# Gated mix of a memory-augmented recurrent attention and an MLP: the columns of queries and exponentials reordered, the reciprocals of the memory rows kept in PSUM, V's matmuls and the side work regrouped

## The chip, the cores and the metric

The kernel runs on one core of a Trainium2 chip. A core has a matmul engine (TensorE, PE in the profile, its weight loads PEld), a vector engine (VectorE, DVE), an engine for activations and copies (ScalarE, ACT), a general engine (GpSimd, POOL) and one that issues transfers (SyncE, SP). SBUF is the working memory of 128 partitions; PSUM is the memory into which matmuls write, in eight banks of 128 x 512 fp32 values. The engines run side by side, each through its own list of instructions in order, and wait for each other on semaphores.

The metric is the time of one execution on the device in microseconds (us). Before the change, three runs took 794.21, 795.08 and 796.0 us, median 795.08.

## The reference, cut to what matters

A sequence x of 2048 tokens of width 512 goes through two branches, mixed by a gate per token:

```python
g = sigmoid((x * gate_w).sum(-1, keepdims=True))
out = g * A(x) + (1 - g) * B(x)

# B: layernorm, 512 -> 1376, gelu, 1376 -> 512
# A: 64 segments of 32 tokens, 32 heads of 128, a memory of 8 rows that is handed on
mem = mem0
for s in range(64):
    h = concat([mem, x[s * 32:(s + 1) * 32]])          # 40 rows
    q, k, v = h @ Wq, h @ Wk, h @ Wv                    # per head
    p = softmax(where(mask, q @ k.T * scale, -1e9))     # 40 x 40 per head
    o = (p @ v) @ Wo                                    # 40 x 512
    mem = o[:8]
    outs.append(o[8:])
```

The mask lets the 8 memory rows see all 40 rows, and a token sees the memory and the tokens of its segment up to itself. Each segment needs the memory of the one before, so the 64 segments follow one another.

## The kernel before, in words

**Two stages.** The first, up to about 100 us, computes the MLP branch with all 128 tokens of a tile at once, stores (1 - g) * B in DRAM (`c_dr`) and loads the attention's weights into SBUF. The second is a loop over the 64 segments `s`; `T, si = divmod(s, 4)` are its tile of 128 tokens and its place in it. The order of the instructions is written out by hand: each engine does its instructions in the order in which the code issues them, and only the waits are added.

**Rows of a segment.** TensorE multiplies with weights of 32 columns at a time, four such groups side by side, one for each quarter of the output's partitions. So 32 of the 40 rows go together: the 8 memory rows and the first 24 tokens (`RIDE`), in `hT`, transposed. The last 8 tokens (`LEFT`) of the four segments of a tile need no memory for their projections; they are gathered as 32 rows (`GL`) and computed a tile ahead as side work: `QL`, `KL` and `VP` hold their queries, keys and values. `prep_h` and `prep_q`, both on POOL, put the tokens of the next segment into `hT` and the left queries of the next segment into `QT`.

**Projections.** A unit (`qk_unit`, `v_unit`) is four matmuls of 128 x 32 weights by 512 columns, side by side. Q and K take four times four units into the banks `U[0]` to `U[3]`; ScalarE casts each bank (`qk_cast`, line 115) and VectorE transposes it in blocks of 32 into `QT` or `KT` (`qk_tr`, line 119). V takes two times four units into `X1` and `X2`, which ScalarE copies (lines 689 and 702).

**Scores and softmax.** The scores of 16 heads lie in the bank `SbF`, those of the other 16 in `W`, with keys on the partitions and 56 columns (`EW`) for each group of four heads. `mask_mm` first writes the mask there through TensorE (line 248); `scores` adds the products: main keys into columns 8 to 48, left keys into columns 0 to 8 and 48 to 56. Before the change the columns are: 0 to 8 memory queries by left keys, 8 to 16 memory queries by main keys, 16 to 40 the 24 tokens, 40 to 48 left queries by main keys, 48 to 56 left queries by left keys. ScalarE takes the exponentials into `E` (`exps`, line 674), the 16 memory columns first and then the 40 others, each for one block of 16 heads.

**Normalising.** Only the memory rows must be right at once. Their sums come from matmuls with a block of ones (`msum`, into columns 320 to 352 of `U[0]` and `U[1]`); `mnorm` takes the reciprocal into `R` (line 681) and multiplies the memory columns of `E` by it (line 682). The other rows are normalised one segment later: `xsums` forms their sums, turned round, with `E` as the weights, in columns 256 to 264 of `SbF`. As left queries have two parts, it makes two passes of eight matmuls (line 605): one with columns 16 to 48 of `E`, one with `EZ`, a copy of columns 48 to 56 that ScalarE makes behind 24 columns of zeros (line 699). `recip_x` takes the reciprocals (line 616), SP stores them in DRAM (`r_dr`) and loads them back on all partitions (`Rb`), POOL adds `R` to a running sum (`racc`, line 621), and `x_norm` multiplies on POOL (line 629) at the start of the next segment, into columns 8 to 32 of `UT` and into `UL`.

**Back to the memory.** `av` multiplies V by `E` into `U`: first the heads of block 0, then those of block 1 (lines 280 and 285). ScalarE copies the memory columns into `UT` (line 712) and the rest into `XR` (line 611). `wo_pass` multiplies `UT` by `Wo` into the whole bank `W` (line 141), ScalarE copies it to `w` (line 635), four matmuls with the selection `SelM` turn the 8 memory rows (line 724), and VectorE casts them into the next `hT` (line 725). That cast is where the next segment's projections can start; segments are counted here from it.

**Side work.** Each segment has up to eight side units (`side`): projections of the next tile's left tokens at `si` 0, 1 and 3, and `Wo` for the last tile's left tokens at `si` 2. `run(W1)`, `run(W2)` and `run(W3)` issue some of them at three places: ahead of `xsums`, ahead of `wo_pass` and behind it; the rest follow the selection. `extra` adds the transposes of a later tile at `si` 3 and, at `si` 0, `out_sel`: it gathers the finished rows of an earlier tile with four matmuls and one of 128 x 128 weights.

The last tile has no next tile, so its segments 60 and 61 have no side units. The last segment, 63, normalises all rows at once and writes the last tile out. The program also tracks the smallest reciprocal and their sum; a slow general version at its end runs only where these leave their bounds.

Of the kernel before, what the change touches and what calls it, by code (L numbers as in the profile page):

```python
# [9 lines left out]
FP32 = mybir.dt.float32  # L10
# [8 lines left out]
MASK_NEG = -1.0e9  # L19
# [8 lines left out]
def kernel(ctx, tc, A_x, A_mem0, A_Wq, A_Wk, A_Wv, A_Wo, A_seg_len, B_x, B_w1, B_b1, B_w2, B_b2, gate_w, out):  # L28
# [89 lines left out]
    def qk_tr(Tb, dst, hf):  # L118
        nc.vector.transpose(out=dst[:, 8 * hf:8 * hf + 8, 0:32, :].rearrange("p a r b -> p a (r b)").bitcast(FP32),  # L119
                            in_=Tb[:].rearrange("p a e b -> p (a e b)").bitcast(FP32))  # L120
# [103 lines left out]
    def out_sel(T, bk):  # L224
# [3 lines left out]
        nc.tensor.matmul(bk[:], lhsT=SelL[:], rhs=wls.pop(T)[:], start=False, stop=True, skip_group_check=True)  # L228
# [36 lines left out]
    def sums(out, E, c_main, c_left, n, start):  # L265
# [3 lines left out]
        for j in range(4):  # L269
            nc.tensor.matmul(out[32 * j:32 * j + 32, :, n - 8:n], lhsT=BO[:, 32 * j:32 * j + 32], rhs=E[:, :, c_left:c_left + 8],  # L270
                             start=False, stop=True, skip_group_check=True, tile_position=(0, 32 * j))
# [20 lines left out]
    with tc.tile_pool(name="mlpw", bufs=1) as mlpw, \  # L292
# [81 lines left out]
        for c in range(4):  # L374
            nc.gpsimd.affine_select(out=SelM[:], in_=SelM[:], pattern=[[-1, M]], compare_op=ALU.not_equal, fill=1.0, base=-32 * c, channel_multiplier=1)
            nc.gpsimd.affine_select(out=SelI[:], in_=SelI[:], pattern=[[-1, 32]], compare_op=ALU.not_equal, fill=1.0, base=-32 * c, channel_multiplier=1)
# [4 lines left out]
        def consts():  # L381
# [5 lines left out]
            nc.vector.tensor_scalar(out=rf[:, 0:1], in0=rf[:, 0:1], scalar1=float(M), scalar2=None, op0=ALU.subtract)  # L387
            nc.vector.tensor_scalar(out=mk1[:], in0=iof[:, 0:4], scalar1=rf[:, 1:2], scalar2=MASK_NEG, op0=ALU.not_equal, op1=ALU.mult)
            yield
            for a in range(4):  # L390
                nc.vector.tensor_scalar(out=Mk[:, a, 16:16 + RIDE], in0=iof[:], scalar1=rf[:, 0:1], scalar2=MASK_NEG, op0=ALU.is_lt, op1=ALU.mult)
                nc.vector.tensor_copy(out=Mk[:, a, 0:8], in_=mk1[:, a:a + 1].to_broadcast([P, 8]))
                nc.vector.tensor_scalar(out=Mk[:, a, 48:56], in0=iof[:, 0:8], scalar1=rf[:, 2:3], scalar2=MASK_NEG, op0=ALU.is_lt, op1=ALU.mult)
                nc.vector.tensor_scalar(out=Mk[:, a, 48:56], in0=Mk[:, a, 48:56], scalar1=mk1[:, a:a + 1], scalar2=None, op0=ALU.add)
# [85 lines left out]
        def first():  # L480
# [3 lines left out]
            dve_q.append(lambda: nc.vector.tensor_copy(out=hT[0][:, :, 0:M], in_=m0p))  # L484
# [112 lines left out]
    EZ = [lp.tile([P, NG, 32], BF16, name=f"EZ{i}") for i in range(2)]  # L597
    for i in range(2):
        nc.gpsimd.memset(EZ[i][:, :, 0:RIDE], 0.0)

    def xsums(s, E):
        for first, src, c0 in ((True, E, 16), (False, EZ[s % 2], 0)):
            for i in range(NG):
                c, h = i % 4, i // 4
                nc.tensor.matmul(xs8[32 * c:32 * c + 32, 4 * h:4 * h + 4], lhsT=src[:, i, c0:c0 + 32], rhs=BO[:, 0:P:32],  # L605
                                 start=first and h == 0, stop=not first, skip_group_check=True, tile_position=(0, 32 * c))

    def x_raw(s):
        XR = cw.tile([P, 4, NG, 32], BF16, tag="XR", name="XR")
        for j in range(4):  # L610
            nc.scalar.copy(out=XR[:, j], in_=U[j][:, 0:NG * 40].rearrange("p (i q) -> p i q", q=40)[:, :, 8:40])  # L611
        XRs[s] = XR

    def recip_x(s):
# [5 lines left out]
        nc.sync.dma_start(Rb[:].rearrange("p r e -> p (r e)"), r_dr[s % 2][:].rearrange("r e -> (r e)").partition_broadcast(P))  # L620
        nc.gpsimd.tensor_tensor(out=racc[:, 0:RW], in0=racc[:, 0:RW], in1=R[:, 0:RW], op=ALU.add)  # L621
        Rbs[s] = Rb

    def x_norm(s):
        T, si = divmod(s, SPT)
        XR, Rb = XRs.pop(s), Rbs.pop(s)[:].rearrange("p (c q) (h j) -> p h j c q", c=4, h=2)
        for out, o, a, b in ((UT[(s + 1) % 2], M, 0, RIDE), (UL[T % 2], LEFT * si, RIDE, 32)):
# [10 lines left out]
    W1, W2, W3 = 2, 2, 2  # L638
    for s in range(nseg):
        T, si = divmod(s, SPT)  # L640
        last = s == nseg - 1
        hc, hn = hT[s % 3], hT[(s + 1) % 3]
        fill = side(T, si)
# [13 lines left out]
        for n, (t, hf) in enumerate(((0, 0), (1, 0), (0, 1), (1, 1))):  # L657
# [14 lines left out]
        def exps(i2, x):  # L672
            c = slice(16, EW) if x else slice(0, 16)
# [220 lines left out]
```

## Time and profile before

| What | Value |
|---|---|
| Median of three runs | 795.08 us (794.21 to 796.0) |
| The profiled execution's own time | 796.19 us |
| Its span, first to last instruction | 794.4 us |
| Granted TensorE clock | 0.998 |
| First and last cast of line 725 | 109.1 and 774.2 us |
| Busy time of PE, ACT, DVE, POOL | 767.9, 539.9, 327.7, 277.8 us |

The profile is one execution. A line of a timeline has a start from the span's beginning and a length in us, the engine, the line of the code, the operation, what is written and read, and how many equal instructions were merged; brackets hold the engine's idle time before it and what ended it. A merged line's length runs to the end of its last instruction. Matmuls are pipelined, so that one lasts 0.38 us while a new unit starts every 0.216 us.

From the first to the last cast of line 725 there are 62 segments in 665.1 us, 10.73 us each. Most single ones stand between 10.64 and 10.66 us; those with an output selection take 10.85; a few are longer.

### The profile page before, as it was taken

To read this page: it belongs to the slowest core of one execution; us is meant where nothing else is said; L and a number is where in the kernel's file an instruction comes from. 1 tells how busy PE (TensorE), PEld (TensorE's weight loads), DVE (VectorE), ACT (ScalarE), POOL (GpSimd) and SP (SyncE) were. 2 spreads that over 40 slices of the span, in tenths; PEclk is the share of its full clock that TensorE was granted. 3 is DMA by queue.
4 is the path that set the end of the run, shared out by engine and by line. 5 is a ranking of instruction groups with operands and counts; after the bars stand their busy time and mean duration, and the time that the engine had idled before them with its cause. 6 is when DMAs were issued, how large, how long until landed. Compare 5 with 4: busy or idle time off the path is not lost.

```text
span 794.4 us, 42412 instructions
## 1 busy us (share of the span) xinstructions
PE 767.9 (97%) x18921; PEld 428.8 (54%) x18950; DVE 327.7 (41%) x1061; ACT 539.9 (68%) x1503; POOL 277.8 (35%) x519
## 2 busy tenths in 40 slices
PE   7999999999999999999999999999999999999996
PEld 5666555555555555555555555555555555555553
DVE  4776344333334343434343333434343434333334
ACT  3666676766777676767776677777677767776663
POOL 3111033343344434234334324443334434332332
PEclk9999999999999999999999999999999999999999
DMA  6779411212111222211121212122221212121211
GB/s 189 265 269 350 142 59 58 74 60 86 60 53 68 77 70 70 77 57 60 60 86 61 86 61 75 46 75 70 78 70 57 62 58 86 61 80 60 71 65 36
DMA packets 46723, 70.49 MB, mean 89 GB/s; under 512 B 12799, under 2 KB 36456, under 8 KB 45000
## 3 DMA queue, kind: packets, MB, share of 16 engines
q1 hardware_dynamic: 45016, 64.97, 25.0%
q8 instruction: 150, 2.46, 1.3%
q0 software_dynamic: 720, 1.97, 0.7%
q10 hardware_dynamic: 800, 0.79, 0.3%
q14 instruction: 37, 0.30, 0.1%
HBM read 59.06 MB, written 4.45 MB: 80 GB/s over the span
## 4 chain that ended last, share of the span: by engine, by line
PE 93%; ACT 4%; issue 1%; DVE 1%; DMA 1%; POOL 0%; SPq 0%; DVEq 0%; POOLq 0%; ACTq 0%
PE U L110 28%; PE X L129 18%; PE W L141 14%; PE X L110 7%; PE U L468 5%; PE U L280 4%; PE X L141 3%; ACT w L635 3%; PE W L462 3%; PE SbF L462 3%; PE W L724 2%; PE U L267 1%; PE SbF L605 1%; PE SbF L256 1%; PE W L248 1%
## 5 line engine op out<-in xcount | busy, mean ns | idle before, releaser
L629 POOL TENSOR_TENSOR UT<-XR,Rb 128x384 bf16<-128x384 bf16 x126 | 140.0, 1132 | 271.8 <-DMA Rb<-r_dr 211.7
L115 ACT CAST Tb<-U 128x512 bf16<-128x512 f32 x258 | 151.0, 585 | 83.2 <-PE U L110 82.7
L110 PEld LDWEIGHTS <-hT 128*32 128x32 bf16 x4096 | 103.9, 97 | 109.7 <-DVE hT L725 19.1
L110 PE MATMUL U<-Wq_sb,hT 128*32 128x512 bf16 x2048 | 132.8, 379 | 1.1 <-DVE hT L725 1.1
L129 PE MATMUL X<-Wv_sb,hT 128*32 128x512 bf16 x2048 | 133.2, 378 | 0.0
L110 PE MATMUL U<-Wk_sb,hT 128*32 128x512 bf16 x2048 | 132.7, 379 | 0.0
L141 PE MATMUL W<-Wo_sb,UT 128*32 128x512 bf16 x2080 | 124.6, 380 | 1.5 <-ACT UT L712 1.2
L725 DVE CAST hT<-W 128x32 bf16<-128x32 f32 x63 | 12.1, 192 | 231.2 <-PE W L724 231.2
L119 DVE STREAM_TRANSPOSE QT<-Tb 128x256 f32<-128x256 f32 x128 | 57.0, 445 | 82.2 <-ACT Tb L115 81.1
L141 PEld LDWEIGHTS <-UT 128*32 128x32 bf16 x2080 | 57.2, 96 | 58.0 <-POOL racc L621 19.0
L119 DVE STREAM_TRANSPOSE KT<-Tb 128x256 f32<-128x256 f32 x128 | 57.0, 445 | 58.2 <-ACT Tb L115 58.2
L611 ACT CAST XR<-U 128x256 bf16<-128x256 f32 x252 | 78.6, 438 | 0.0
L635 ACT CAST w<-W 128x512 bf16<-128x512 f32 x65 | 38.0, 585 | 45.2 <-PE W L141 45.2
L629 POOL TENSOR_TENSOR UL<-XR,Rb 128x128 bf16<-128x128 bf16 x126 | 60.4, 500 | 0.0
L712 ACT CAST UT<-U 128x64 bf16<-128x64 f32 x252 | 35.3, 227 | 31.3 <-PE U L285 31.3
L129 PEld LDWEIGHTS <-hT 128*32 128x32 bf16 x2048 | 45.2, 95 | 20.7
L681 DVE RECIPROCAL R<-U 128x32 f32<-128x32 f32 x126 | 45.0, 357 | 25.9 <-PE U L270 23.0
L621 POOL TENSOR_TENSOR racc<-racc,R 128x72 f32<-128x72 f32 x63 | 21.2, 336 | 97.9 <-DVE R L616 95.2
L468 PE MATMUL U<-w_sb,hTm 128*128 128x512 bf16 (+1 forms) x163 | 49.5, 381 | 0.6
L115 ACT CAST Tb<-X 128x512 bf16<-128x512 f32 x62 | 36.5, 589 | 16.4 <-PE X L110 16.4
L462 PEld LDWEIGHTS <-w_sb 128*128 128x128 bf16 (+1 forms) x352 | 34.7, 102 | 21.1 <-issue 4.0
L256 PEld LDWEIGHTS <-KT 128*32 128x32 bf16 x2048 | 33.7, 95 | 16.3 <-DVE KT L119 0.2
(158 smaller groups left out, 1176.0 us busy)
## 6 DMA issues: line engine op xcount, KB each, us to landing
Rb<-r_dr SPq DMA_DIRECT2D x63, 512.0 KB, 3.9
Wv_sb<-in_A_Wv_dram SPq DMA_DIRECT2D x4, 1024.0 KB, 7.0
Wq_sb<-in_A_Wq_dram SPq DMA_DIRECT2D x4, 1024.0 KB, 7.2
Wk_sb<-in_A_Wk_dram SPq DMA_DIRECT2D x4, 1024.0 KB, 10.7
Wo_sb<-in_A_Wo_dram SPq DMA_DIRECT2D x4, 1024.0 KB, 14.8
VP<-VL SPq DMA_DIRECT2D x64, 64.0 KB, 3.0
xt<-in_A_x_dram SPq DMA_DIRECT2D x16, 128.0 KB, 2.7
xs<-in_A_x_dram SPq DMA_DIRECT2D x16, 128.0 KB, 2.3
```

What stands on the lines that cost most here:

```text
L110: nc.tensor.matmul(bk[32 * j:32 * j + 32, :], lhsT=G[:, kc, :], rhs=W5[t][:, kc, h0:h1, j, :], start=(kc == 0), stop=(kc == KC - 1), tile_ ...
L115: nc.scalar.copy(out=Tb[:], in_=bk.rearrange("p (a b e) -> p a e b", a=8, b=2))
L119: nc.vector.transpose(out=dst[:, 8 * hf:8 * hf + 8, 0:32, :].rearrange("p a r b -> p a (r b)").bitcast(FP32), in_=Tb[:].rearrange("p a e b ...
L129: nc.tensor.matmul(bk[32 * j:32 * j + 32, :], lhsT=G[:, kc, :], rhs=Wv5[:, kc, 4 * vb:4 * vb + 4, j, :], start=(kc == 0), stop=(kc == KC - ...
L141: nc.tensor.matmul(bk[32 * c:32 * c + 32, :], lhsT=U_[:, j, i, :], rhs=Wo_sb[:, 4 * i + j, :], start=(n == 0), stop=(n == NW - 1), tile_po ...
L256: nc.tensor.matmul(Sb[i2][32 * j:32 * j + 32, i - 4 * i2, M:M + 40], lhsT=KT[:, h // 2, :, h % 2], rhs=QT[:, h // 2, :, h % 2], start=Fals ...
L462: nc.tensor.matmul(hp[:rows, 0:TB * P], lhsT=w1_sb[:, kc, fc * P:fc * P + rows], rhs=yTs[blk][:, kc, :], start=(kc == 0), stop=(kc == KC - 1))
L468: nc.tensor.matmul(bp(blk, tt)[:], lhsT=hTm[blk % 2][:rows, fc, tt * P:(tt + 1) * P], rhs=w2_sb[:rows, fc, :], start=(fc == 0), stop=(fc = ...
L611: nc.scalar.copy(out=XR[:, j], in_=U[j][:, 0:NG * 40].rearrange("p (i q) -> p i q", q=40)[:, :, 8:40])
L629: nc.gpsimd.tensor_tensor(out=out[:, :, 4 * h:4 * h + 4, o:o + b - a], in0=XR[:, :, 4 * h:4 * h + 4, a:b], in1=Rb[:, h, :, :, a:b], op=ALU ...
L635: nc.scalar.copy(out=w[:], in_=W[:])
L681: nc.vector.reciprocal(out=r, in_=U[i2][:, 320:352])
```

## The change

The diff does five things.

**Order of queries.** The columns of `hT`, `QT` and `E` turn round: the 8 left queries first, then the 24 tokens, then the 8 memory rows. `hT` holds the tokens in columns 0 to 24 and the memory in 24 to 32; `QT` the left queries in 0 to 8. `E` then has left queries by left keys in 0 to 8, left queries by main keys in 8 to 16, the tokens in 16 to 40, and the memory queries in 40 to 56. The masks, the selection `SelI`, the copies from `U` and the two products of `x_norm` follow. In `xsums` the first 8 rows are the left queries, so the second pass takes columns 0 to 8 of `E` itself as weights of eight columns; `EZ`, its memsets and its copy go.

**Reciprocals of the memory rows.** `mnorm` writes them into columns 288 to 320 of `SbF` and of `W` (`RP`) and multiplies from there. `recip_x` copies both into `R` with two more VectorE instructions, behind the issue of the two transfers and ahead of POOL's sum.

**Masks.** `mask_mm(1)` moves from behind the first projection to behind the first block's scores. The first block's exponentials become one instruction of all 56 columns.

**V's units.** Of the second half of V, the second unit moves behind the second block's scores, and the last one behind `msum(1)` and `mnorm(1)`.

**Side work.** `W1, W2, W3` depend on `si`: (2, 2, 2) at 0 and 3, (1, 2, 3) at 1 and 2. `out_sel` does its last matmul as four of 32 columns side by side.

```diff
-    def qk_tr(Tb, dst, hf):
-        nc.vector.transpose(out=dst[:, 8 * hf:8 * hf + 8, 0:32, :]...
+    def qk_tr(Tb, dst, hf, c0=0):
+        nc.vector.transpose(out=dst[:, 8 * hf:8 * hf + 8, c0:c0 + 32, :]...
...
-        nc.tensor.matmul(bk[:], lhsT=SelL[:], rhs=wls.pop(T)[:], start=False, stop=True, skip_group_check=True)
+        wl = wls.pop(T)
+        for si in range(SPT):
+            nc.tensor.matmul(bk[32 * si:32 * si + 32, :], lhsT=SelL[:, 32 * si:32 * si + 32], rhs=wl[:], start=False, stop=True,
+                             skip_group_check=True, tile_position=(0, 32 * si))
...
-        nc.gpsimd.tensor_copy(out=hT[s % 3][:, :, M:32], in_=xTs[T][:, :, seg * si:seg * si + RIDE])
+        nc.gpsimd.tensor_copy(out=hT[s % 3][:, :, 0:RIDE], in_=xTs[T][:, :, seg * si:seg * si + RIDE])
...
-        nc.gpsimd.tensor_copy(out=QT[:, :, 32:40, :].bitcast(FP32),
+        nc.gpsimd.tensor_copy(out=QT[:, :, 0:LEFT, :].bitcast(FP32),
...
+    RP = [bk[:, 288:320] for bk in (SbF, W)]
...
-            nc.gpsimd.affine_select(out=SelI[:], in_=SelI[:], pattern=[[-1, 32]], ...
+            for q0, a, b in ((0, RIDE, 32), (LEFT, 0, RIDE)):
+                nc.gpsimd.affine_select(out=SelI[:, a:b], in_=SelI[:, a:b], pattern=[[-1, b - a]], ...
...
-        for first, src, c0 in ((True, E, 16), (False, EZ[s % 2], 0)):
+        for first, c0, n in ((True, 8, 32), (False, 0, LEFT)):
             for i in range(NG):
                 c, h = i % 4, i // 4
-                nc.tensor.matmul(xs8[32 * c:32 * c + 32, 4 * h:4 * h + 4], lhsT=src[:, i, c0:c0 + 32], rhs=BO[:, 0:P:32],
+                nc.tensor.matmul(xs8[32 * c:32 * c + n, 4 * h:4 * h + 4], lhsT=E[:, i, c0:c0 + n], rhs=BO[:, 0:P:32],
...
+        for i2 in (1, 0):
+            nc.vector.tensor_copy(out=R[:, 32 * i2:32 * i2 + 32], in_=RP[i2])
         nc.gpsimd.tensor_tensor(out=racc[:, 0:RW], in0=racc[:, 0:RW], in1=R[:, 0:RW], op=ALU.add)
...
-    W1, W2, W3 = 2, 2, 2
+    WS = ((2, 2, 2), (1, 2, 3), (1, 2, 3), (2, 2, 2))
...
             if n == 0:
                 flush(act_q, 9)
-                mask_mm(1)
                 flush(dve_q, 9)
-            qk_tr(qk_cast(bk[:]), (QT, KT)[t], hf)
+            qk_tr(qk_cast(bk[:]), (QT, KT)[t], hf, LEFT * (1 - t))
...
-            c = slice(16, EW) if x else slice(0, 16)
+            c = slice(0, 40) if x else slice(40, EW)
...
-            r, e = R[:, 32 * i2:32 * i2 + 32], E[:, 4 * i2:4 * i2 + 4, 0:16].rearrange("p i (a q) -> p i a q", q=8)
+            r, e = RP[i2], E[:, 4 * i2:4 * i2 + 4, 40:56].rearrange("p i (a q) -> p i a q", q=8)
...
         scores(s, 0)
-        for i2 in range(2):
-            exps(0, i2)
+        mask_mm(1)
+        nc.scalar.activation(out=E[:, 0:4, :], in_=Sb[0], func=ACTF.Exp, scale=scale)
         for kc in range(KC):
             v_unit(X1, hc, 0, kc)
         nc.scalar.copy(out=v_out(V, 0), in_=X1[:])
...
             msum(0)
             mnorm(0)
-        v_unit(X2, hc, 1, 1)
         scores(s, 1)
         for i2 in range(2):
             exps(1, i2)
+        for kc in range(1, 3):
+            v_unit(X2, hc, 1, kc)
         if not last:
-            nc.scalar.copy(out=EZ[s % 2][:, :, RIDE:32], in_=E[:, :, 48:56])
-        for kc in range(2, KC):
-            v_unit(X2, hc, 1, kc)
+            msum(1)
+            mnorm(1)
+        v_unit(X2, hc, 1, 3)
         nc.scalar.copy(out=v_out(V, 1), in_=X2[:])
         if last:
             break
-        msum(1)
-        mnorm(1)
         run(W1)
```

More of the change, by code (lines that the diff above doesn't have):

```diff
@@ L610, in x_raw @@
         for j in range(4):
-            nc.scalar.copy(out=XR[:, j], in_=U[j][:, 0:NG * 40].rearrange("p (i q) -> p i q", q=40)[:, :, 8:40])
+            nc.scalar.copy(out=XR[:, j], in_=U[j][:, 0:NG * 40].rearrange("p (i q) -> p i q", q=40)[:, :, 0:32])
         XRs[s] = XR
@@ L642 @@
         hc, hn = hT[s % 3], hT[(s + 1) % 3]
+        W1, W2, W3 = WS[si]
         fill = side(T, si)
@@ L711 @@
         for j in (0, 2, 1, 3):
-            nc.scalar.copy(out=UT[s % 2][:, j, :, 0:M], in_=U[j][:, 0:NG * 40].rearrange("p (i q) -> p i q", q=40)[:, :, 0:8])
+            nc.scalar.copy(out=UT[s % 2][:, j, :, 0:M], in_=U[j][:, 0:NG * 40].rearrange("p (i q) -> p i q", q=40)[:, :, 32:40])
         x_raw(s)
@@ L733 @@
     nx = slice(8 * NG, 40 * NG)
-    sums(xsum, E, 16, 48, 32, True)
+    sums(xsum, E, 8, 0, 32, True)
     for _ in out_sel(T - 1, X2):
```

32 lines of the change are left out of this document (15 added, 17 removed).

## The prediction

> **What bounds the kernel now.** I read the page's first part, then windows cut at the casts of line 725 (one per segment), then the timeline of one ordinary segment. Part 1 points to TensorE:
>
> ```profile
> PE 767.9 (97%) x18921; PEld 428.8 (54%) x18950; DVE 327.7 (41%) x1061; ACT 539.9 (68%) x1503; POOL 277.8 (35%) x519
> ```
>
> The ends of matmuls are modelled, so this busy time also covers waits. The windows show it (start:end, length, then busy time and count of each engine):
>
> ```profile
> 742.28:752.93 10.65, 9.66 (x264) 5.31 (x257) 3.40 (x12) 7.31 (x22) 4.03 (x7) 1.00 0.27 79
> 731.64:742.28 10.64, 10.46 (x288) 5.60 (x284) 3.39 (x11) 7.65 (x22) 4.04 (x7) 1.00 0.26 80
> ```
>
> The first is segment 60, which has no side units; the second, segment 59, has eight, some 1.7 us of matmuls. Both take 10.65 us. So a chain of waits sets a segment, and the side units lie in its gaps: matmul time counts only on that chain. Segment 33 (start, length, engine, line):
>
> ```profile
> 458.21 0.58 ACT L689 CAST V<-X 128x512 bf16<-128x512 f32 x1
> ...
> 458.48 0.27 PE L256 MATMUL W<-QT,KT 128*32 128x40 bf16 x16
> ...
> 458.86 0.42 ACT L674 ACTIVATE E<-W 128x64 bf16<-128x64 f32 x2
> ...
> 459.14 0.20 PE L267 MATMUL U<-E,BO 128*32 128x32 bf16 x4
> ...
> 459.31 0.24 ACT L699 COPY EZ<-E 128x64 bf16<-128x64 bf16 x1
> ...
> 459.42 0.36 DVE L681 RECIPROCAL R<-U 128x32 f32<-128x32 f32 x1 [0.18 <-PE U L270]
> 459.46 0.58 ACT L702 CAST V<-X 128x512 bf16<-128x512 f32 x1
> ...
> 459.88 0.23 DVE L682 TENSOR_TENSOR E<-E,R 128x64 bf16<-128x64 bf16 x1
> ...
> 460.10 0.23 PEld L280 LDWEIGHTS <-V 32*128 32x128 bf16 x16
> ...
> 460.16 0.28 PE L280 MATMUL U<-E,V 32*128 32x40 bf16 x16
> ...
> 463.47 0.26 PE L724 MATMUL W<-SelM,w 128*128 128x8 bf16 x4 [0.16 <-ACT w L635]
> ...
> 463.83 0.19 DVE L725 CAST hT<-W 128x32 bf16<-128x32 f32 x1 [3.61 <-PE W L724]
> ```
>
> The chain: V's first copy holds ACT, the memory columns' exp of the second block follows, then sums, reciprocal, multiplication, and the second half of A times V at 460.16. From there to the selection at 463.47 it is 3.31 us, with side units or without. The second half waits for two things: the multiplication (459.88 + 0.23 = 460.11) and V's second copy (459.46 + 0.58 = 460.04, weights loaded from 460.10). The multiplication is last, by only about 0.05 us. That margin is the case.
>
> **The change, part by part**, in the times of segment 33.
>
> *Second scores one V unit earlier.* A unit is four matmuls; units start 0.216 us apart. The scores move from 458.48 to 458.26. Their exp started 0.28 after their last matmul, so they allow 458.65; ACT is held by V's copy of 458.21, and after a 512-wide cast the next ACT instruction starts 0.48 later (457.22 to 457.70 in this segment), so 458.69: 0.17 earlier. The transposed K they read was ready at 457.84 + 0.45 = 458.29; as the mask matmuls (0.095 us, 454.31 to 454.41) now stand behind the first scores, the last three projections, their casts and transposes come 0.095 earlier: 458.19, and 0.05 for the load is 458.24. Just in time. V's first copy stays, as the same matmuls stand before it.
>
> *V's last unit behind the memory sums.* exp 0.22 (458.92), sums 0.05 later (458.97; before 459.08 to 459.14). The unit follows 0.05 on (459.02), its last matmul starts 0.02 later, takes 0.38, and ACT follows after 0.05: 459.47, where the copy starts today. 0.58 and 0.06 for loading the weights give 460.11 for the second half, against 460.16. The multiplication, 0.17 earlier, would allow 459.99. So V's copy is what is late next, and of 0.17 us gained only 0.047 remains (unrounded), in 63 segments: **-3.0 us**.
>
> *No EZ copy, one exp for the first block.* 0.244 us of ACT go (63 times), but V's second copy then waits for its matmuls instead: nothing gained beyond the above. The joined exp: 0.230 and 0.312 for 64 and 160 columns give 0.37 for 224; from 457.61 it ends at 457.98, with 0.23 us to its sums at 458.21. Nothing; without that cover it costs the 0.14 it adds to the first part.
>
> *xsums with eight columns.* The second pass (0.05 us) lies between half and double that, so -0.03 to +0.05. With W1 = 2, TensorE reaches the second half at 459.02 + 3 x 0.216 + 0.10 + 0.10 (the change to 32-row tiles, as now) + 0.14 = 460.01; with W1 = 1, at 459.79. Cover 0.10: nothing.
>
> *Reciprocals in PSUM.* No row shows VectorE writing a reciprocal to PSUM or multiplying with a PSUM operand. Single-input rows show no surcharge for reading PSUM (L763, one element from PSUM, 147 ns; L758, from SBUF, 146); the wide L232, with a PSUM operand, takes 745 against 687 for L447, without one. So -0.06 to +0.06 for each of the two; I take 0, as small rows are nearer. Spare is 0.12 (459.99 to 460.11). [...]
>
> The multiplication L682 takes 0.224 at least and 0.545 at most, long where it meets POOL's multiplications, while L681, which reads PSUM, never exceeds 0.359 beside the same work. In eight segments the stretch reached the chain, 0.02 to 0.14 each. With R in PSUM I expect the multiplication to act like L681: between 0 and -0.5 us, I take **-0.5**. [...]
>
> *Two copies of the reciprocals into R*, 0.19 each by L725 (the same 128x32 from PSUM): 460.2 to 460.6, behind L616. The next on VectorE is L725, after 3.6 us idle. wo_pass overwrites bank W from 460.87 and needs the first copy, some 460.4: 0.4 spare. POOL's accumulation waits about 0.3 longer; behind it stand prep_q, 0.42, and the next prep_h, 0.27, done by 461.7; x_norm starts at the earliest 1.3 us into the next segment. SP's r_dr store is issued before the copies, so nothing is late there. Cost 0; without cover 0.4 each segment.
>
> *Side units (1, 2, 3).* One unit of si 1 and 2 moves from W1, where V's copy is waited for anyway, to the wait for w. Three units from 462.69 plus 0.12 for the change to 128-wide tiles end at 463.46, the selection starts at 463.47. 0 to +0.02, taken as 0. Two units still follow it.
>
> *Output selection* (14 segments): 409.12 to 409.68 now; two groups of 0.216 and one tile change of 0.1 make 0.53: -0.03 each, **-0.4** (0 to -1.4). The reordered columns move the same bytes: 0. Setup: four selects of 0.2 on POOL, whose memsets of hTm then end near 7.1 us and are read at 21.8; EZ's memsets go. The last segment gains 0.1, its exp being 0.12 earlier.
>
> Sum -3.0 - 0.5 - 0.4 - 0.1 = -4.0. The profiled execution took 796.19 (span 794.4, 1.8 around it): 792.2. The median of the three runs is 1.1 below it, so against 795.08: **791.1**.
>
> **Rivals.**
> 1. *The exp does not move up*, because its scores wait for K or ACT longer. Then V's last unit, now behind the sums, is late: 459.14 + 0.05 + 0.02 + 0.38 + 0.05 = 459.64 and the second half at 460.28, 0.12 later, 63 times: +7.6, 802.7. It decides once the exp starts after 458.74. For it: K is just in time. Against it: all three releases come 0.095 to 0.22 earlier.
> 2. *The margin is eaten*: my 0.047 is a difference of sums of five latencies; 0.05 too little leaves the side gains alone, 794.1. For it: the just-in-time places. Against it: every latency is a repeated row.
> 3. *PSUM slows the reciprocal and the multiplication by twice my bound*, 0.24 together: 460.23, +0.07, 799.5. Against it: the small rows.
> 4. *V's copy is not last*, the multiplication sets the end: 0.17 x 63, 783.4. Against it: the weights' load at 460.10.
>
> **How the numbers follow.** A measurement of this kernel tells 0.2% (1.6 us) from no change. Forecast 0.52 (its own range 789.5 to 793.2: 0.03 to 0.065 a segment and the side gains); rival 2 0.23; rival 1, wholly or in part, 0.14; rival 3 0.06; rival 4 0.05. Faster: forecast, rival 4 and a little of rival 2, 0.59; same, the rest of rival 2 and small parts of 1 and 3, 0.23; slower 0.18. The range, 789 to 797, takes in the forecast, rival 2 and the mild part of rivals 1 and 3.
>
> **What the profile will show.** Right: ordinary segments near 10.60; the exp of the second block 5.51 us after the segment's cast instead of 5.68; V's second copy still at 6.28; the loads of V last before the second half, the multiplication done 0.1 before; L682 never above 0.3. Wrong: segments of 10.65 or more, the second copy of V after 6.33, or wo_pass waiting for VectorE.

## The result and the profile after

The changed kernel takes 792.94 us (median of nine runs, 791.85 to 793.21), the kernel before 795.48 beside it (nine runs, 794.21 to 796.36). The ratio is 0.9968, 95% interval 0.9960 to 0.9977: faster by 2.5 us (1.8 to 3.2). The forecast was 791.1, a gain of 4.0; the gain is there, smaller.

The profiled execution took 792.61 us, its span is 790.8, 3.6 below the 794.4 of before. Part 1 of the page:

```profile
PE 772.0 (98%) x18995; PEld 426.8 (54%) x18995; DVE 338.6 (43%) x1188; ACT 520.6 (66%) x1376; POOL 278.2 (35%) x521
```

ScalarE has lost 19 us of work and 127 instructions (the copies into `EZ` and the second exp of the first block), VectorE has won 11 us and 127 instructions (126 of them the copies into `R`). Neither is what the time follows. The windows of segments 59 and 60, cut at the casts of line 734 (725 before):

```profile
727.85:738.49 10.64, 10.49 (x288) 5.75 (x284) 3.65 (x14) 7.35 (x20) 4.04 (x7) 1.00 0.16 50
738.49:749.09 10.60, 9.76 (x268) 5.12 (x260) 3.55 (x13) 7.00 (x20) 4.03 (x7) 1.00 0.26 87
```

As before, the segment with eight side units and the one with none take about the same time: the chain of waits still sets it. Segment 33 shows the chain (its first cast at 450.29; start, length, engine, line):

```profile
455.32 0.58 ACT L699 CAST V<-X 128x512 bf16<-128x512 f32 x1 [0.24 <-PE X L129]
...
455.37 0.27 PE L262 MATMUL W<-QT,KT 128*32 128x40 bf16 x16
...
455.80 0.43 ACT L684 ACTIVATE E<-W 128x64 bf16<-128x64 f32 x2
...
456.08 0.20 PE L273 MATMUL U<-E,BO 128*32 128x32 bf16 x4
...
456.44 0.37 DVE L691 RECIPROCAL W<-U 128x32 f32<-128x32 f32 x1
...
456.58 0.58 ACT L713 CAST V<-X 128x512 bf16<-128x512 f32 x1 [0.35 <-PE X L129]
...
456.84 0.22 DVE L692 TENSOR_TENSOR E<-E,W 128x64 bf16<-128x64 bf16 x1
...
457.11 0.14 DVE L629 COPY R<-W 128x32 f32<-128x32 f32 x1
457.17 0.18 DVE L629 COPY R<-SbF 128x32 f32<-128x32 f32 x1
457.22 0.17 PEld L286 LDWEIGHTS <-V 32*128 32x128 bf16 x16 [0.17 <-ACT V L713]
...
460.54 0.26 PE L733 MATMUL W<-SelM,w 128*128 128x8 bf16 x4
...
460.90 0.19 DVE L734 CAST hT<-W 128x32 bf16<-128x32 f32 x1 [3.55 <-PE W L733]
```

In us after the segment's cast, with the forecast in the middle:

| Step | before | forecast | after |
|---|---|---|---|
| exp of the second block's memory columns | 5.68 | 5.51 | 5.51 |
| their sums | 5.96 | 5.79 | 5.80 |
| V's second copy | 6.28 | 6.28 | 6.29 |
| multiplication ends | 6.92 | 6.76 | 6.77 |
| second half of A times V | 6.98 | 6.93 | 6.93 |
| selection | 10.29 | 10.24 | 10.25 |
| next cast | 10.65 | 10.60 | 10.61 |

The exp comes 0.17 us earlier, the sums 0.16, the second half 0.04. The idle time in front of its weights is now put down to V's copy (`[0.17 <-ACT V L713]`): the wait has passed from the multiplication to ScalarE's copy, and the multiplication is done 0.16 us before the second half starts. Before, the second half followed it by 0.05, so that some 0.11 us are to spare now.

Where the profile's 3.6 us come from: between the first and the last cast of the loop the 62 segments take 661.57 us instead of 665.14. The median of a segment falls from 10.650 to 10.610 (with an output selection from 10.854 to 10.813), 0.041 x 62 = 2.5. The other 1.0 are single long segments: in sum 2.3 us above the medians before, 1.2 after. Of the difference, 0.5 are eight segments of before in which VectorE's multiplication was stretched; most of the rest are stalls of TensorE in single segments, to which the last experiments turn. One is VectorE's: in segment 56 the cast of line 734 starts 0.42 us behind the semaphore instruction ahead of it instead of 0.06, and the segment takes 11.16. The runs below with the reciprocals in PSUM show it too, at the same instruction, which has 1343 recorded VectorE instructions ahead of it (semaphore instructions counted); those with them in SBUF don't. In the kernel before, the second multiplication of segment 4 starts as late, 0.42 us behind its semaphore instruction, with 319 ahead of it. Both counts are 63 over a multiple of 256. That would fit borders like those that the last experiments find in TensorE's instructions, but no run tested it for VectorE. Each of the two profiles is one execution; the medians of the runs tell of 2.5.

### The profile page after: what moved, and what is told of

Same layout as the page of the kernel before. It is cut to its first block, busy times and chain, and to the rows that moved or that the text cites. A ratio compares the mean times of both kernels' runs of the same rounds, so it can differ in the third digit from the quotient of the medians.

```text
span 790.8 us, 42774 instructions
## 1 busy us (share of the span) xinstructions
PE 772.0 (98%) x18995; PEld 426.8 (54%) x18995; DVE 338.6 (43%) x1188; ACT 520.6 (66%) x1376; POOL 278.2 (35%) x521
## 3 DMA queue, kind: packets, MB, share of 16 engines
q8 instruction: 150, 2.46, 1.3%
## 4 chain that ended last, share of the span: by engine, by line
PE 92%; DVE 3%; DMA 2%; issue 1%; ACT 1%; POOL 1%; DVEq 0%; SPq 0%; POOLq 0%; ACTq 0%
PE U L110 28%; PE X L129 17%; PE W L141 14%; PE X L110 7%; PE U L477 5%; PE X L141 4%; PE U L286 3%; PE W L471 3%; PE SbF L471 3%; DVE W L691 1%; PE W L733 1%; PE U L273 1%; DVE R L623 1%; PE W L262 1%; PE SbF L262 1%
## 5 line engine op out<-in xcount | busy, mean ns | idle before, releaser
L110 PEld LDWEIGHTS <-hT 128*32 128x32 bf16 x4096 | 104.2, 97 | 117.4 <-DVE hT L734 19.5
L129 PE MATMUL X<-Wv_sb,hT 128*32 128x512 bf16 x2048 | 145.7, 379 | 0.0
L129 PEld LDWEIGHTS <-hT 128*32 128x32 bf16 x2048 | 53.2, 95 | 20.4
L477 PE MATMUL U<-w_sb,hTm 128*128 128x512 bf16 (+1 forms) x176 | 52.5, 382 | 0.0
L713 ACT CAST V<-X 128x512 bf16<-128x512 f32 x64 | 37.4, 585 | 22.2 <-PE X L129 22.1
L699 ACT CAST V<-X 128x512 bf16<-128x512 f32 x64 | 37.4, 585 | 15.6 <-PE X L129 15.6
```

The costliest lines, as they stand in the source:

```text
L110: nc.tensor.matmul(bk[32 * j:32 * j + 32, :], lhsT=G[:, kc, :], rhs=W5[t][:, kc, h0:h1, j, :], start=(kc == 0), stop=(kc == KC - 1), tile_ ...
L129: nc.tensor.matmul(bk[32 * j:32 * j + 32, :], lhsT=G[:, kc, :], rhs=Wv5[:, kc, 4 * vb:4 * vb + 4, j, :], start=(kc == 0), stop=(kc == KC - ...
L477: nc.tensor.matmul(bp(blk, tt)[:], lhsT=hTm[blk % 2][:rows, fc, tt * P:(tt + 1) * P], rhs=w2_sb[:rows, fc, :], start=(fc == 0), stop=(fc = ...
L699: nc.scalar.copy(out=v_out(V, 0), in_=X1[:])
L713: nc.scalar.copy(out=v_out(V, 1), in_=X2[:])
```

## Experiments

All ratios are to the kernel before, run on the same chip; times are medians. "Segment" is the median of an ordinary one.

| Run | us | ratio (95%) | segment |
|---|---|---|---|
| the change | 792.94 | 0.9968 (0.9960 to 0.9977) | 10.610 |
| order alone, on the kernel before | 792.73 | 0.9972 (0.9963 to 0.9982) | 10.61 |
| masks alone, on the kernel before | 794.66 | one run | 10.650 |
| mask back | 794.59 | 0.9991 (0.9982 to 1.0000) | 10.633 |
| V's last unit ahead of the sums | 792.54 | 0.9959 (0.9946 to 0.9973) | 10.603 |
| reciprocals in SBUF | 793.16 | 0.9970 (0.9960 to 0.9980) | 10.61 |
| padded copy back | 793.07 | 0.9962 (0.9948 to 0.9975) | 10.61 |
| side units (2, 2, 2) | 791.68 | one run | 10.61 |
| output selection in one matmul | 792.85 | one run | 10.61 |

### The order alone, and the masks alone

The kernel before, with only the masks moved and V's units regrouped; `EZ`, the exps, `R` in SBUF and the side units stay.

```diff
-                mask_mm(1)
...
+        mask_mm(1)
...
-        v_unit(X2, hc, 1, 1)
...
-        for kc in range(2, KC):
+        for kc in range(1, 3):
             v_unit(X2, hc, 1, kc)
+        if not last:
+            msum(1)
+            mnorm(1)
+        v_unit(X2, hc, 1, 3)
...
-        msum(1)
-        mnorm(1)
```

> The kernel before with only the order of the change: masks behind the first block's scores, second scores one V unit earlier, V's last unit behind the sums. Column order, EZ, reciprocals in R, two exponentials for the first block, side units (2, 2, 2) and the output selection stay as they were. Theory (the order alone brings the gain): ordinary segments 10.61 instead of 10.65, with the second exp at 5.515 and V's second copy at 6.29; -2.6 us, less what stretched multiplications cost, which mostly hide now: about 793. Rival (the regrouping only works with the freed ACT or TensorE time): segments between 10.63 and 10.65, 794 or more.

Segment 33 of this run (its first cast at 451.06):

```profile
456.58 0.43 ACT L673 ACTIVATE E<-W 128x64 bf16<-128x64 f32 x2
...
457.36 0.58 ACT L705 CAST V<-X 128x512 bf16<-128x512 f32 x1
457.60 0.23 DVE L681 TENSOR_TENSOR E<-E,R 128x64 bf16<-128x64 bf16 x1
...
457.99 0.17 PEld L280 LDWEIGHTS <-V 32*128 32x128 bf16 x16
```

Exp at 5.515, V's second copy from 6.294 to 6.879, segments 10.61: step for step the changed kernel. The multiplication still takes up to 553 ns (545 before), and in five segments this makes the second half late, by 0.2 us in all. So the order of TensorE's instructions brings all of the gain that the median shows; nothing else in the diff is needed for it. With `mask_mm(1)` moved and nothing else:

> The kernel before with only the masks moved behind the first block's scores. Theory (before, the second scores wait for TensorE and not for K, which is ready 0.19 us earlier): segments stay at 10.65. Rival (the masks' place gains by itself): 10.63 or less.

Segments stay at 10.650. In the kernel before, K is ready 0.19 us earlier than the scores that read it; an earlier K alone serves nobody.

### The mask back behind the first projection

```diff
             if n == 0:
                 flush(act_q, 9)
+                mask_mm(1)
                 flush(dve_q, 9)
...
-        mask_mm(1)
```

> The changed kernel with mask_mm(1) back behind the first projection. Theory (the transposed K is just in time for the second block's scores): K is ready 0.095 us later, at 5.10, the scores start at 5.17 to 5.19 instead of 5.08, their exp at 5.55 to 5.58 instead of 5.515, and all behind it follows: segments of 10.65 to 10.67, +2.5 to +4.1 us, so the whole gain is gone: about 796. Rival (the masks' place is of no account, as TensorE does the same matmuls ahead of V's first copy): no change, 793.

The same segment 33, its first cast at 450.31:

```profile
455.35 0.59 ACT L699 CAST V<-X 128x512 bf16<-128x512 f32 x1
...
455.47 0.28 PE L262 MATMUL W<-QT,KT 128*32 128x40 bf16 x16
...
455.86 0.42 ACT L685 ACTIVATE E<-W 128x64 bf16<-128x64 f32 x2
...
456.63 0.58 ACT L713 CAST V<-X 128x512 bf16<-128x512 f32 x1 [0.35 <-PE X L129]
```

The scores start at 5.16 instead of 5.08, the exp at 5.55, V's copy at 6.32, and segments take 10.633: 0.024 longer, a little under the expectation of 0.04 or more, for of the 0.08 lost at the scores 0.05 were spare against ScalarE, and the exp was 7 ns shorter. Read with the run before: the masks are worth nothing by themselves, but without them six tenths of a segment's gain are gone, for K is just in time. The regrouping keeps 0.017 of 0.041 us without the masks; the whole gain needs both.

### V's last unit ahead of the sums

If V's second copy is what is late, then its last unit should stand ahead of the sums after all, while the multiplication has time to spare.

```diff
-        for kc in range(1, 3):
+        for kc in range(1, KC):
             v_unit(X2, hc, 1, kc)
         if not last:
             msum(1)
             mnorm(1)
-        v_unit(X2, hc, 1, 3)
```

> The changed kernel with V's last unit ahead of msum(1) again instead of behind it. Theory (in the changed kernel V's second copy is the last wait of the second half of A times V; the multiplication is done 0.11 us before): the unit's matmuls end earlier, the copy of V starts at 6.09 us after the segment's cast instead of 6.29 and is no longer last; the sums start at 5.85 instead of 5.80, the multiplication ends at 6.82, the second half starts at 6.875 instead of 6.934. Ordinary segments 10.55 instead of 10.61, in all -3.8 us: about 789. Rival (the order of V's units has given what it can, another wait stands right behind): no change, 793. Second rival (the later sums are what counts): +0.05 a segment, 796.

Segment 33 of this run (its first cast at 449.49):

```profile
455.59 0.58 ACT L712 CAST V<-X 128x512 bf16<-128x512 f32 x1 [0.15 <-PE U L276]
...
455.75 0.37 DVE L691 RECIPROCAL W<-U 128x32 f32<-128x32 f32 x1 [0.25 <-PE U L276]
...
456.15 0.22 DVE L692 TENSOR_TENSOR E<-E,W 128x64 bf16<-128x64 bf16 x1
...
456.43 0.28 PE L286 MATMUL U<-E,V 32*128 32x40 bf16 x16
```

V's copy comes 0.2 earlier, at 6.10, and is done at 6.68. But the sums end later, the reciprocal starts at 6.26 instead of 6.15, and the multiplication is done at 6.88 instead of 6.77. The second half starts at 6.93, as in the changed kernel; segments take 10.603, a gain of 0.006. Moving the unit swaps which of the two is last, and the end is the same to 0.01. So the earlier scores and the masks carry the gain, and V's last unit may stand on either side of the sums. The multiplication had been expected at 6.82, 0.06 earlier: of that, 0.047 lie between the sums and the reciprocal, 0.398 us against 0.351, with four matmuls of 512 columns running ahead of the sums instead of behind them. Why that costs so much was not followed further.

### The reciprocals in SBUF

```diff
-        for i2 in (1, 0):
-            nc.vector.tensor_copy(out=R[:, 32 * i2:32 * i2 + 32], in_=RP[i2])
...
-            r, e = RP[i2], E[:, 4 * i2:4 * i2 + 4, 40:56]...
+            r, e = R[:, 32 * i2:32 * i2 + 32], E[:, 4 * i2:4 * i2 + 4, 40:56]...
```

> The changed kernel with the reciprocals of the memory rows in R in SBUF again, without the two copies. Theory: single multiplications are stretched again, up to 0.55 us, where POOL multiplies at the same time; but the multiplication now has 0.11 us to spare before V's copy, so little of it reaches the chain: 0 to +0.2 us in all, 793; ordinary segments 10.61. Rival (the place in PSUM carries a good part of the gain by itself): segments longer by 0.02 or more, +1.3 us or more. Second rival (the two copies hold up POOL or wo_pass in the changed kernel): faster than it by 1 us or more.

The multiplication's line, least, median and longest in ns, in the changed kernel:

```profile
L692 DVE TENSOR_TENSOR E<-E,SbF x63: 220/221/222, 104.0 to 765.5; 128x64 bf16<-128x64 bf16 x63
L692 DVE TENSOR_TENSOR E<-E,W x63: 220/221/222, 104.7 to 766.2; 128x64 bf16<-128x64 bf16 x63
```

and in this run:

```profile
L690 DVE TENSOR_TENSOR E<-E,R x126: 224/225/546, 103.4 to 766.3; 128x64 bf16<-128x64 bf16 x126
```

With the reciprocals in PSUM 22 of the 126 multiplications run beside one of POOL's, and none takes more than 222 ns. With them in SBUF 15 do, and 11 of these take 267 to 546; in the kernel before it was 19 of 29. The time is the same, though: 793.16. In four segments (6, 31, 33 and 45) a long first multiplication makes the second one start 0.13 to 0.21 late and the second half 0.02 to 0.10: 0.2 us in all, where eight segments lost 0.5 before. In the changed kernel no segment loses any to it. So by these traces the order, with some 0.11 us in front of the second half, takes the larger part of this gain, and the place in PSUM some 0.2 us, too little to be seen in the medians of the runs.

### The side steps

Three edits for which the forecast had terms. The copy into `EZ` and the second pass of 32 columns are put back:

```diff
-        for first, c0, n in ((True, 8, 32), (False, 0, LEFT)):
+        for first, src, c0 in ((True, E, 8), (False, EZ[s % 2], 0)):
...
+            nc.scalar.copy(out=EZ[s % 2][:, :, 0:LEFT], in_=E[:, :, 0:LEFT])
```

> The changed kernel with the padded copy EZ made again by ACT behind the exponentials and used by the second pass of xsums with 32 columns. Theory (V's second copy waits for its matmuls until 6.29 us, the padded copy lies before it from 5.94 to 6.18): segments stay at 10.61, no change, 793. Rival (the removed ACT work and the narrower pass were part of the gain): up to 0.24 us of ACT or 0.05 us of TensorE a segment, +3 to +15 us.

V's second copy at 6.294, segments 10.61: a quarter of a microsecond of ScalarE per segment, given back, costs nothing. The side units at (2, 2, 2) in every segment:

```diff
-    WS = ((2, 2, 2), (1, 2, 3), (1, 2, 3), (2, 2, 2))
+    WS = ((2, 2, 2), (2, 2, 2), (2, 2, 2), (2, 2, 2))
```

> The changed kernel with side units (2, 2, 2) in all segments. Theory (the unit moved from W1 to W3 lies beside V's copy in the one place and beside the cast of w in the other): segments with si 1 and 2 stay at 10.61. Rival (it mattered at one of the two places): at least 0.02 longer or shorter there, those with si 0 and 3 unchanged.

Ordinary segments 10.606 to 10.610 at every `si`, 10.811 with an output selection: nothing. The output selection's last matmul as one of 128 x 128:

```diff
-        for si in range(SPT):
-            nc.tensor.matmul(bk[32 * si:32 * si + 32, :], lhsT=SelL[:, 32 * si:32 * si + 32], ...
+        nc.tensor.matmul(bk[:], lhsT=SelL[:], rhs=wls.pop(T)[:], ...
```

> The changed kernel, with the output selection's last matmul as one of 128 x 128 again. Theory A (the prediction's term): the selection of si 0 is 0.03 later than in the changed kernel and the 14 segments with an output selection take 10.84 instead of 10.813, +0.4 us in all. Rival B (from the profile after: the stretch from A times V to the selection of si 0 is 3.517 against 3.525 before): 10.81 to 10.82, at most 0.1 us in all.

From the second half of A times V to the selection 3.529 us against 3.517, segments with an output selection 10.815 against 10.813. The four matmuls side by side save 0.01 us, not 0.03, and the segment 0.002: the forecast's -0.4 is 0.0. The stretch in the changed kernel, segment 44:

```profile
577.35 0.40 PE L226 MATMUL U<-w,SelR 128*32 128x512 bf16 x4
...
577.57 0.40 PE L230 MATMUL U<-wl,SelL 128*32 128x512 bf16 x4
...
577.90 0.26 PE L733 MATMUL W<-SelM,w 128*128 128x8 bf16 x4
```

The two groups are 0.216 us apart, and the selection of the memory rows comes 0.335 behind the second: 0.216 and 0.119 for the change from 32-wide to 128-wide weights. Together it is 0.551, against 0.562 with one matmul of 128 x 128. That change of width now stands directly ahead of the four short matmuls, and the second of them comes 0.039 us behind the first instead of 0.028, which takes back another 0.011.

### A further step: wo_pass in two halves

From the second half of A times V to the selection it is 3.3 us of which ScalarE's copy of the whole bank `W` is 0.59. Two halves of 256 columns, the second into `U[0]`, let the first be copied while the second is multiplied.

```diff
-        for n in range(NW):
-            wo_group(W, U_, n)
...
-        nc.scalar.copy(out=w[:], in_=W[:])
+        for bk, d0, d1 in ((W, 0, Dm // 2), (U[0], Dm // 2, Dm)):
+            for n in range(NW):
+                wo_group(bk, U_, n, d0, d1)
+            nc.scalar.copy(out=w[:, d0:d1], in_=bk[:, 0:d1 - d0])
...
-    WS = ((2, 2, 2), (1, 2, 3), (1, 2, 3), (2, 2, 2))
+    WS = ((3, 2, 1), (2, 2, 2), (2, 2, 2), (3, 2, 1))
```

> The changed kernel with the pass over Wo in two halves of 256 columns, the second one in the bank U[0], each with its own ACT cast, and side units (3, 2, 1) at si 0 and 3, (2, 2, 2) at 1 and 2. Theory (all from the second half of A times V to the cast of line 734 is on the chain, and the cast of w, 0.585 us, stands in it whole): behind the second half only a cast of 256 columns is left, 0.38 us by the 256-column rows, so the selection comes 0.21 earlier at si 1 and 2: 10.40. At si 0 and 3 the third unit at W1 makes TensorE reach the second half of A times V 0.11 later and the selection 0.2 earlier: about -0.10 each. In all -9 us, 784. Rival (TensorE's own work becomes the bound, or the 64 shorter matmuls take longer than 32 long ones): segments of 10.55 or more, 790 or more.

Measured: 789.34 us (788.21 to 793.06, five runs), ratio 0.9923 (0.9908 to 0.9938): 3.6 us better than the change and the best of the study, but not the 9 expected. The profiled execution, 793.06, is the slowest of the five. Undisturbed segments of `si` 1 and 2 take 10.40, 0.21 less, as expected. At `si` 0 and 3 the three units ahead of the second half delay it from 6.93 to 7.06, so that undisturbed ones take 10.76 and 10.55, some 0.05 less instead of 0.10, and many segments are long without any such reason. First the units:

> wo_pass in two halves as in the run before, but the side units (2, 2, 2) at every si. Theory A (at si 0 and 3 the three units ahead of the second half of A times V hold it up): the second half starts 6.93 us after the cast instead of 7.05, wo_pass at 7.65 instead of 7.79, and these 30 segments are some 0.14 shorter each: -4 us against the run with (3, 2, 1), about 785. Rival B (the units are only moved: what they no longer hold up ahead of the second half, they hold up between the two halves of wo_pass and the selection): wo_pass at 7.65, but the selection of si 0 still at 10.40 and the time within 1 us of the run with (3, 2, 1), about 789. Both: segments of si 2 stay at 10.40.

With (2, 2, 2) everywhere the second half is at 6.93 and `wo_pass` at 7.65 in all segments, and the selection at `si` 0 is later still, 10.47 against 10.40: rival B, the delay only moved. The time was 795.49 (792.47 to 799.02, ratio 1.0004), 6 us worse, which neither expected. Its profiled execution was the quickest of its ten, so that no trace shows where the slower ones lost their time; that stays open.

### The sudden stalls

Segment 7 of the changed kernel takes 11.03 us instead of 10.61. Its second half of A times V, in the timeline:

```profile
179.42 0.14 PEld L286 LDWEIGHTS <-V 32*128 32x128 bf16 x10
179.42 0.24 PE L286 MATMUL U<-E,V 32*128 32x40 bf16 x9
...
179.92 0.22 PE L286 MATMUL U<-E,V 32*128 32x40 bf16 x7 [0.26 <-issue]
179.92 0.11 PEld L286 LDWEIGHTS <-V 32*128 32x128 bf16 x6 [0.37 <-issue]
```

Nine of sixteen equal matmuls, a hole, and the other seven, with nothing waited for that the profile shows ("issue"). The queues' part of the page, of the change and of the two halves:

```profile
q8 instruction: 150, 2.46, 1.3%
```

```profile
q8 instruction: 167, 2.74, 1.3%
```

2.46 MB in 150 packets is 16,384 bytes each; TensorE's 37,990 recorded instructions (18,995 loads and as many matmuls) make 253 a packet, 42,150 in the other kernel 252. So I counted the recorded TensorE instructions ahead of each stall, plus one per segment (which an instruction that is not recorded would explain), modulo 256. A stall is here a gap between two matmuls over 0.06 us above the median of its place, in the segments 3 to 59 that have the usual number of matmuls; gaps that follow within 0.75 us count with it. In the change four of five stand at 179 or 180, in the run with V's last unit ahead five of five, with the output selection in one matmul six of seven and the seventh at 178, in the two halves 26 of 28 at 178 to 180. To test it, matmuls that repeat the first mask were put ahead of the first segment:

```diff
-    mask_mm(0)
+    for _ in range(17):
+        mask_mm(0)
```

> The changed kernel with the mask matmuls ahead of the first segment issued 17 times instead of once: 128 more TensorE instructions (weight loads and matmuls), 1.6 us of work before the segments, nothing within them. In the traces so far, the sudden stalls of TensorE in single segments come where the number of recorded TensorE instructions before them, plus one per segment, is 179 or 180 over a multiple of 256; one 16,384-byte packet of the instruction queue stands for 256 instructions of 64 bytes. Theory A (the stalls belong to the borders between blocks of 256 instructions): the stalls keep the count of 179 or 180 in this run too, so that they fall elsewhere in the segments; none is left at si 3 between 7.0 and 7.7 us after the cast, where four of the changed kernel's stood. Rival B (they belong to that place of the segment, to its transfers or waits): they stay at si 3 between 7.0 and 7.7, with counts near 51. Both: ordinary segments 10.61, si 0 10.81, and the time about 794.5, the 1.6 us more, with up to 1.5 either way for the stalls.

Segment 5 of this run, `si` 1:

```profile
158.99 0.12 PEld L286 LDWEIGHTS <-V 32*128 32x128 bf16 x7 [0.17 <-ACT V L714]
158.99 0.22 PE L286 MATMUL U<-E,V 32*128 32x40 bf16 x6
...
159.43 0.24 PE L286 MATMUL U<-E,V 32*128 32x40 bf16 x10 [0.23 <-issue]
159.43 0.14 PEld L286 LDWEIGHTS <-V 32*128 32x128 bf16 x9 [0.33 <-issue]
```

The stalls have left `si` 3, where every segment now takes 10.60 to 10.61, and stand at `si` 1 (five) and 2 (one). All six have the count 166 or 167. That is not the 179 expected, but this trace lacks 13 matmul records ahead of the segments (163 of one line instead of 176), and with them it is 179 and 180; rival B's 51 is far off. The time was 793.98 (ratio 0.9982, 0.9971 to 0.9994), 1.0 more than the change with 1.6 us of work added. The same on the two halves, with 25 mask calls:

> wo_pass in two halves with side units (3, 2, 1) at si 0 and 3 (the version at 789.34), with the mask matmuls ahead of the first segment issued 25 times: 192 more TensorE instructions, 2.4 us of work ahead of the segments. Theory A (block borders): the stalls keep the count of 179 or 180; the borders that fell at si 1 and 3 between 7.8 and 8.9 us, inside wo_pass, fall some 64 instructions later, behind or at the end of wo_pass, and those at si 2 near 7.0 fall into wo_pass; the sum of what segments take above the median of their si, 4.8 us in the profile of the version without the shift, changes by more than 1 us in one direction or the other; time between 788 and 794. Rival B (place or transfers): stalls stay at si 1 and 3 between 7.8 and 8.9, the sum stays, and the time is 789.3 + 2.4 = 791.7.

798.71 us (ratio 1.0038, 1.0026 to 1.0049): worse than either bound. 36 of its 38 stalls stand at 165 to 167 (again 13 records are missing), and now at `si` 0 and 2 near 7.0 to 7.7 as well as at `si` 1 and 3 near 9; the time above the medians is 11.1 us instead of 4.8. These medians hold stalls themselves, as many segments of `si` 1 and 3 have one; from the first cast to the last the two profiled executions take 661.55 and 665.49 us, 3.9 more. Where the borders fall was theory A's; that it could cost this much was neither's. So with 192 instructions ahead of the loop, and nothing changed within it, the median of the runs rose by 9.4 us, of which about 2.4 are the work added. Between the two profiled executions it is 5.9, for the one without the shift was the slowest of its five. These five differ by 4.9 us with the same instructions, so the place of the borders isn't all. What the two halves gain hangs on where their borders happen to lie, and need not outlive a change ahead of the loop.

The traces also keep the start and the length of every packet of the instruction queue, so that the stalls can be set beside them. Between 140 and 735 us of the change, TensorE crosses 125 borders (counted as above), and exactly one packet ends between one border and the next. The 121 quiet borders are crossed 1.4 to 4.7 us after the last packet ended, median 2.8; the four at which a stall ends, 1.2 to 1.7. In the two halves it is 1.2 to 1.6 at 26 stalls and a median of 2.3 elsewhere, with the 192 instructions ahead 1.2 to 1.7 at 36 stalls and 2.0 elsewhere. No border in these three traces is crossed earlier than 1.2 us after a packet's end. So the stalls stand where the packet came last, which fits TensorE waiting there for its next instructions. At the four stalls of the change the two borders are 3.1 to 3.6 us apart, at the quiet ones 4.8 in the median: where matmuls are short, 256 instructions are used up sooner. Short blocks also pass quietly: 21 of the 121 quiet borders come 3.0 to 3.6 us after the one before; what sets the start of a packet was not followed.

## Why the prediction was right, and where its sizes were off

**The bound.** "A chain of waits sets a segment, and the side units lie in its gaps": the runs with the side units and the padded copy show it. One moves a unit of TensorE's work, the other adds 0.24 us of ScalarE's, and both leave 10.61.

**The main step** came as worked out: the exp 0.17 earlier, the sums 0.16, V's copy where it was to 0.01, V's loads last before the second half. The forecast put the second half at 6.93 (460.11 in segment 33), and it starts at 6.934; V's copy is 7 ns longer than before, 585 for 578, and starts 10 ns later. So 0.041 of 0.047 per segment remained: -2.5 for -3.0. Rival 1 (the exp doesn't move) fell in the change, and the run with the mask back shows how near it was: 0.08 at the scores give back 0.024 of 0.041. Rival 4 (V's copy isn't last, the multiplication sets the end, 783.4) fell with the result, where the second half's loads wait for V's copy. Its 783.4 can't be had by freeing that copy either: in the run of V's last unit that gains 0.006, because the multiplication then stands right behind.

**EZ, the joined exp, xsums, the copies into R:** nothing, as forecast. The copies took 0.14 and 0.18, not 0.19 each, and `wo_pass` did not wait for VectorE. The joined exp took 0.363 for the estimated 0.37.

**PSUM's price.** I had bounded each of the two instructions by 0.06 and taken 0. The reciprocal takes 367 ns into PSUM and 358 into SBUF, the multiplication 221 ns with a PSUM operand and 225 without: +0.009 and -0.004, on the side of the small rows. Rival 3 has nothing left.

**The stretched multiplication, -0.5:** gone in the trace, as forecast (222 at most). But the term did not stand by itself. The run with the reciprocals in SBUF keeps stretches of 546, and only 0.2 us of them reach the chain in its trace; the medians of the runs can't tell 793.16 from 792.94. The forecast gave the spare of 0.12 in one place and counted the stretches in another; with that spare, a delay of up to 0.12 is free in either version. The larger part of the 0.5 belongs to the order, some 0.2 to the reciprocals in PSUM, as far as one trace of each tells.

**The output selection, -0.4,** is the term that failed: 0.01 of 0.03 in TensorE, 0.002 in the segment. The forecast put 0.1 for the change of width and got 0.53; the change to 128-wide weights takes 0.119, as its own paragraph on the side units had it (0.12), so that it is 0.551. The rest went to the slower start of the four matmuls behind that change. **The last segment's -0.1** can't be told: from the last cast to the end it is 20.2 us before and 20.5 after, and 20.1 to 20.5 in the other runs without the two halves.

So -3.0 was -2.5, -0.5 came in the profile, the larger part of it through the order, and -0.4 was nothing. The profile's 3.6 also hold about half a microsecond of other single stalls, most of which the borders of the instruction stream would explain; the median of the runs, -2.5, is the ordinary segments'.

## What to carry to other kernels

When two waits end within 0.05 us of each other, an earlier one is worth only the distance to the other: work out what is late next, and expect a swap of the two to give nothing, as V's last unit did (0.006 us a segment). An edit can be worth nothing alone and more than half of the gain beside another (the masks, beside the regrouped V units: 0.024 of 0.041 us a segment), so undo and add each by itself before one is kept or dropped. In a long unrolled program, compare ordinary segments by their median before the total: with the borders 192 instructions further on, the segments of the two halves took 665.49 us instead of 661.55 (one execution each), 3.9 more, where the edits brought 2.5.

## What the runs showed of the hardware

**Borders of the instruction stream.** TensorE's sudden stalls (0.12 to 0.43 us for the four of the change that stand at 179 or 180) come at nearly one count of its instructions modulo 256, and not at every such border. From one border to the next the instruction queue brings one packet of 16,384 bytes, at all 125 borders between 140 and 735 us of the change. The change has some 150 such packets and five visible stalls, the two halves 167 and 28. The four at 179 or 180 make their segments 0.05 to 0.42 us longer, some 0.7 us of 790 together; in the worst run here the time above the medians is 11.1 us. A stall ends 1.2 to 1.7 us after the queue's last packet did, at quiet borders this distance is 2.0 to 2.8 in the median. Why the packets come late at some borders is open.

**A wait that moves.** With the reciprocals in PSUM, in a bank that ScalarE reads as well, the reciprocal starts 0.351 us after the sums instead of 0.282. A semaphore instruction now stands ahead of it each time:

```profile
L691 DVEq EVENT_SEMAPHORE  x126: 21/21/21, 103.5 to 765.8; - x126
```

In the run with the reciprocals in SBUF, as in the kernel before, it stood ahead of the multiplication:

```profile
L690 DVEq EVENT_SEMAPHORE  x126: 21/21/21, 103.3 to 766.3; - x126
```

From the reciprocal's end to the multiplication it is 0.033 now and was 0.105. From the sums to the multiplication's end the two versions take 0.972 and 0.968 us. So a second wait seems to cost VectorE some 0.07, on whichever of the two instructions it stands; no run has it on neither.
